# Down projection of an adaLN block: first inner product copied into the second's PSUM bank, residual gated once, and the last outer product of group 1 split by seven

## The chip, the cores and the metric

The kernel runs on one core of one Trainium2 chip. The metric is the device time of one execution in microseconds (us). The kernel before has a median of 729.99 us over three runs (731.19, 729.23, 729.99). The execution that was profiled took 729.17 us, and its span, from its first to its last instruction, is 727.4 us. Engines are named as in the profile: PE (TensorE matmuls), PEld (its weight loads), DVE (VectorE), ACT (ScalarE), POOL (GpSimd) and SP (SyncE, which here only issues DMAs).

## The reference

One transformer block on 2048 tokens of width 1024, with adaptive layer norms, linear attention of 32 heads and a gated feed-forward of inner width 3584. All inputs are bf16.

```
mod = silu(c) @ w_mod                        # six rows of 1024: sa, ca, ga, sb, cb, gb
h = layernorm(x) * (1 + ca) + sa
q, k, v = h @ wqkv ; pq, pk = phi(q), phi(k)
o = (pq @ (pk^T v)) / (pq . sum(pk))         # per head
x = x + ga * (o @ wo)
h = layernorm(x) * (1 + cb) + sb
x = x + gb * ((gelu(h @ w_gate) * (h @ w_up)) @ w_down)
```

The change is in the last line: the product with `w_down`, its gate `gb`, and the sum with `x`.

## The kernel before, in words

**Phases.** `kvq_phase` makes keys, values and queries, `merge_phase` and `wo_phase` the attention output and the first residual sum, which goes to the output tensor in HBM (`x2_scr`, a view of it). The feed-forward then runs for two groups of 1024 tokens: `gate_up(0)`, `down_out(0)`, `gate_up(1)`, `down_out(1)`.

**Products by seven.** A matrix product cut into 2x2 quadrants is computed with seven quadrant products instead of eight, on sums of quadrants of the two factors (the Strassen-Winograd scheme). In `down_out(g)` the activations of the group are cut into quadrants of 512 tokens by 1792 inner elements, and `w_down` into quadrants of 1792 by 512 columns. The seven outer products are called `b11`, `b21`, `t0`, `t1`, `b22`, `t2`, `t3`. Each of them is computed in one of two ways:

- `plain` (L1951): four row tiles of 128 tokens, each 14 matmuls of 128 x 512 into one PSUM bank, 56 wide matmuls in all.
- `nested` (L1986): again by seven, steps `g1` to `g7`, each 14 matmuls of 256 columns (two token tiles by seven inner tiles), 98 narrow matmuls in all.

Before, `t1` and `t3` of group 0 and `t3` of group 1 are plain, and all others are nested. The `t3` of group 1 is the last product of the kernel. Its fourth row tile is cut into 256, 128 and 128 columns, and the two 128-column parts go to other banks, to which ACT copies what the bank already holds (L1969).

**Steps of a nested product.** `g1` makes the first product in a bank `a`, and `fcopy` (L1097) has ACT copy it to SBUF in fp32. `g2` makes the second product in a bank of its own and hands both to `out`, where DVE adds them (`tt_op`, L791). `g3`, `g5` and `g6` continue in bank `a`, `g4` and `g7` use a bank `c`; ACT copies the results of `g3` and `g5` to SBUF, and DVE adds them in.

**What `out` does with a result.** The outer seven are joined in two fp32 tiles of SBUF, `p1v` and `p5v`, in PSUM banks 0 to 3 (into which ACT copies a partial sum so that a later plain product adds to it), and in the functions `c11_out`, `c12_out`, `c22_quads`, `c21_last`, `c21_out`. They multiply with a row of `gb` (`gate2`, `gbrow`) and either send the result to HBM with an accumulating DMA of the POOL queue (`added` and `send`, L1934), which adds it to the residual there, or, for the last 512 tokens, add it to residual rows that were loaded (`rest`, L1942) and store with a DMA of the ACT queue (`store`, L1947). Before, the gated value of a partial sum is kept too (`w12`, which lies in `p1v`) and added to the gated rest, so that `u2_out` and `u2_quads` gate once and `c12_out` gates again.

**Weight sums.** Nested products need sums of quadrants of `w_down` and of its outer sums. For the products in `LATER` (L1344) they are made in HBM (`v_scr`) by DMAs of the POOL queue, half of them accumulating (`wd_later`, L1403). They are issued piece by piece in `gate_up`, each batch behind a small POOL copy that waits for a weight load (`wd_moves`, L1353); `MOVE_AT` (L1765) has the units n of `gate_up` in which one is issued. SP loads the operands of each product into slots of SBUF (`quarters`, `W_AT`, L1910), in the order of its queue, as soon as the slot's last reader is done.

**The order of the work.** All instructions are first recorded, then put in order by a planner (`Plan`, L216), and then each engine's sequence is permuted by a table of shifts written out in the file (`SHIFTS`, L20 to L208, applied in `refine`, L470). Each engine executes its own sequence in order.

Of the kernel before, what the change touches and what calls it, by code (L numbers as in the profile page):

```python
# [11 lines left out]
BF16 = mybir.dt.bfloat16  # L12
# [495 lines left out]
def kernel(  # L508
# [1258 lines left out]
    def gate_up(g, before=()):  # L1767
# [26 lines left out]
        for n in range(NU):  # L1794
# [49 lines left out]
            if n == 0:  # L1844
                wd_todo.extend(wd_later(LATER[g + 1]))
# [390 lines left out]
```

## Time and profile before

The times are in us of the profiled execution.

| | |
|---|---|
| profiled execution | 729.17 (median of the runs 729.99) |
| span | 727.4, granted TensorE clock 1.000 |
| PE busy | 717.1 (99%), 4504 matmuls |
| DVE busy | 662.3 (91%) |
| ACT busy | 461.5 (63%) |
| POOL busy | 133.3 (18%) |
| HBM | read 128.91 MB, written 41.55 MB |
| start of `down_out(0)`, of `gate_up(1)`, of `down_out(1)` | about 402, 474, 643 |

The times of the stages in the last row are where the first matmuls of the lines L2008 and L1728 stand in the chain that ended last. Busy time of PE is the union of its matmuls; between matmuls that follow each other closely nothing is counted as idle. DVE, ACT and POOL have the line of a helper for most of their work (L791, L1097), so they are told apart by shapes and times.

### The profile page before, as it was taken

To read this page: it belongs to the slowest core of one execution; us is meant where nothing else is said; L and a number is where in the kernel's file an instruction comes from. 1 tells how busy PE (TensorE), PEld (TensorE's weight loads), DVE (VectorE), ACT (ScalarE), POOL (GpSimd) and SP (SyncE) were. 2 spreads that over 40 slices of the span, in tenths; PEclk is the share of its full clock that TensorE was granted. 3 is DMA by queue.
4 is the path that set the end of the run, shared out by engine and by line. 5 is a ranking of instruction groups with operands and counts; after the bars stand their busy time and mean duration, and the time that the engine had idled before them with its cause. 6 is when DMAs were issued, how large, how long until landed. Compare 5 with 4: busy or idle time off the path is not lost.

```text
span 727.4 us, 12503 instructions
## 1 busy us (share of the span) xinstructions
PE 717.1 (99%) x4504; PEld 417.8 (57%) x4515; DVE 662.3 (91%) x1457; ACT 461.5 (63%) x841; POOL 133.3 (18%) x210
## 2 busy tenths in 40 slices
PE   8999999999999999999999999999999999999997
PEld 4444445454444455555555787655555555568885
DVE  6698988898889999999989999898888899989998
ACT  5584665679777889998877742036777767651220
POOL 2241832011030033532221000031022100000011
PEclk9999999999999999999999999999999999999999
DMA  9967597998999797996999999786237733599994
GB/s 309 328 203 231 135 174 150 328 369 250 298 286 247 255 274 181 303 277 192 302 201 229 282 276 289 244 161 149 82 105 196 179 72 117 155 276 255 285 264 107
DMA packets 183854, 163.94 MB, mean 225 GB/s; under 512 B 34864, under 2 KB 164144, under 8 KB 183792
## 3 DMA queue, kind: packets, MB, share of 16 engines
q1 hardware_dynamic: 156880, 121.45, 57.8%
q0 software_dynamic: 25344, 40.38, 23.3%
q10 hardware_dynamic: 1568, 1.31, 0.6%
q8 instruction: 35, 0.57, 0.3%
q14 instruction: 27, 0.22, 0.1%
HBM read 128.91 MB, written 41.55 MB: 234 GB/s over the span
## 4 chain that ended last, share of the span: by engine, by line
PE 94%; DVE 2%; POOL 2%; ACT 1%; issue 1%; DMA 0%; DVEq 0%; ACTq 0%
PE psum L1728 34%; PE psum L2008 16%; PE psum L1739 11%; PE psum L1160 7%; PE psum L1230 7%; PE psum L1959 5%; PE psum L1542 4%; PE psum L1608 3%; PE psum L1259 2%; PE psum L926 2%; PE psum L1274 1%; POOL mem L877 1%; PE psum L808 1%; DVE mem L791 1%; DMA mem<-in_A_x_dram 0%
## 5 line engine op out<-in xcount | busy, mean ns | idle before, releaser
L791 DVE TENSOR_TENSOR mem<-mem 128x512 f16<-128x512 f16 (+11 forms) x837 | 383.4, 501 | 11.4 <-ACT mem L1097 2.3
L1728 PE MATMUL psum<-mem 128*128 128x512 f16 x1144 | 272.9, 379 | 0.0
L1097 ACT ACTIVATE mem<-psum 128x512 f32<-128x512 f32 (+3 forms) x327 | 171.5, 554 | 137.3 <-PE psum L2008 49.4
L791 DVE TENSOR_TENSOR mem<-psum,mem 128x512 f16<-128x512 f32 (+5 forms) x225 | 167.2, 750 | 24.4 <-PE psum L1160 4.8
L1728 PEld LDWEIGHTS <-mem 128*128 128x128 f16 (+1 forms) x1144 | 111.8, 98 | 102.7 <-issue 0.2
L2008 PE MATMUL psum<-mem 128*128 128x256 f16 (+1 forms) x1078 | 119.6, 273 | 0.0
L2008 PEld LDWEIGHTS <-mem 128*128 128x128 f16 x1078 | 105.5, 98 | 14.3
L1739 PE MATMUL psum<-mem 128*128 128x256 f16 x742 | 106.0, 273 | 0.0
L1739 PEld LDWEIGHTS <-mem 128*128 128x128 f16 (+1 forms) x742 | 72.4, 98 | 41.2 <-DVE mem L791 0.2
L1160 PE MATMUL psum<-mem 128*128 128x512 f16 (+1 forms) x273 | 62.4, 379 | 1.4 <-ACT mem L1266 0.5
L1934 POOL DMA_DIRECT2D out_dram<-mem x12 | 14.6, 1414 | 218.3 <-DVE mem L791 218.3
L1230 PE MATMUL psum<-mem 128*128 128x512 f16 x224 | 51.5, 379 | 0.0
L791 DVE TENSOR_TENSOR psum<-psum,mem 128x256 f32<-128x256 f32 x106 | 44.5, 427 | 7.5 <-ACT mem L1097 5.6
L1160 PEld LDWEIGHTS <-mem 128*128 128x128 f16 x280 | 27.2, 98 | 33.0 <-issue 1.6
L1785 ACT ACTIVATE psum<-psum 128x512 f32<-128x512 f32 x56 | 32.6, 585 | 14.7 <-PE psum L1739 8.5
L1804 ACT ACTIVATE mem<-psum 128x512 f16<-128x512 f32 x56 | 32.7, 596 | 12.3 <-PE psum L1728 12.1
L1959 PE MATMUL psum<-mem 128*128 128x512 f16 (+2 forms) x196 | 38.0, 349 | 0.0
L1230 PEld LDWEIGHTS <-mem 128*128 128x128 f16 (+1 forms) x224 | 21.6, 98 | 26.1 <-issue 0.8
L1814 ACT ACTIVATE mem<-mem 128x512 f16<-128x512 f16 x56 | 34.8, 629 | 0.3 <-DVE mem L791 0.3
L1259 PE MATMUL psum<-mem 128*128 128x512 bf16 x124 | 28.7, 379 | 1.4 <-DMA mem<-in_A_wqkv_dram 1.0
L1338 POOL DMA_DIRECT2D ts<-in_B_w_down_dram x28 | 27.6, 1165 | 11.1 <-DMA ts<-in_B_w_down_dram 11.0
L1542 PE MATMUL psum<-mem 128*128 128x512 f16 x128 | 28.3, 379 | 0.0
(148 smaller groups left out, 608.9 us busy)
## 6 DMA issues: line engine op xcount, KB each, us to landing
mem<-in_B_w_gate_dram SPq DMA_DIRECT2D x14, 1024.0 KB, 8.1
mem<-in_B_w_up_dram SPq DMA_DIRECT2D x14, 1024.0 KB
mem<-in_w_mod_dram SPq DMA_DIRECT2D x24, 512.0 KB, 7.8
mem<-us SPq DMA_DIRECT2D x24, 448.0 KB, 6.1
mem<-vs SPq DMA_DIRECT2D x20, 448.0 KB, 7.7
mem<-in_B_w_down_dram SPq DMA_DIRECT2D x18, 448.0 KB, 6.9
ts<-in_B_w_down_dram POOLq DMA_DIRECT2D x28, 256.0 KB, 5.7
mem<-ts SPq DMA_DIRECT2D x15, 448.0 KB, 8.7
```

The costliest lines, as they stand in the source:

```text
L791: ve.tensor_tensor(out=out, in0=a, in1=b, op=op)
L1097: ac.activation(out=t, in_=ps, func=AF.Copy)
L1160: te.matmul(ps, lhsT=A[:, k, i * P:(i + 1) * P], rhs=B[:, k, :], start=(start and k == 0), stop=(k == KH - 1), skip_group_check=True)
L1230: te.matmul(o, lhsT=W[:, k, (j0 + i) * P:(j0 + i + 1) * P], rhs=h_form(a, k), start=(start and k == 0), stop=(k == KH - 1), skip_group_che ...
L1259: te.matmul(ps, lhsT=hr1[b][:, k, tl * P:(tl + 1) * P], rhs=Wk[:, k, n * NW:(n + 1) * NW], start=(k == 0), stop=(k == KD - 1))
L1542: te.matmul(psw[:, half, :], lhsT=pqT[b][:, g, tl * P:(tl + 1) * P], rhs=Wp[:, g, half * NW:(half + 1) * NW], start=(g == 0), stop=(g == K ...
L1728: te.matmul(ps, lhsT=a[:, k, e, :], rhs=b[:, k, :], start=(start and k == 0), stop=(k == KH - 1), skip_group_check=True)
L1739: te.matmul(ps, lhsT=self.x[a][:, k, :], rhs=self.y[y][:, k, :], start=(start and k == 0), stop=(k == KH // 2 - 1), skip_group_check=True)
L1804: ac.activation(out=o, in_=ps, func=AF.Gelu_apprx_tanh)
L1814: ac.activation(out=o, in_=o, func=AF.Gelu_apprx_tanh)
L1959: te.matmul(psm[:, b, c], lhsT=A[:, i, q * P:(q + 1) * P], rhs=wt[:, i, c], start=(start and i == 0), stop=(i == NPR - 1), skip_group_chec ...
L2008: te.matmul(ps[:, q, :], lhsT=a[:, k, q * P:(q + 1) * P], rhs=y[:, k, :], start=(start and q == 0 and k == 0), stop=(k == NPR // 2 - 1), s ...
```

## The change

In both down phases:

- `g1` of a nested product takes a second bank `b`, and ACT copies the first product from bank `a` to bank `b`. `g2` adds its own product to that bank. DVE no longer adds the two, and the copy to SBUF is gone.
- `u2_out` and `u2_quads` no longer gate and no longer refill PSUM banks; `c12_out` adds the partial sum first and gates the sum once; `w12` is gone.

In group 1 alone:

- `t3` is nested. `sub_sums` on `A22` makes its left sums on DVE (four instructions of 128 x 1792), `v_scr` has a fourth part, and `MOVE_AT` issues 16 moves instead of 8 in `gate_up(1)`, over the units 1 to 12. Seven operand loads of 448 KB replace two of 896 KB.
- The product `t2` (`c22_quads`) no longer loads its residual and stores, but sends its result with two accumulating DMAs. Of `t3`, the first quadrant is sent in the same way (one DMA of 128 KB), the second and third are stored by half width.
- The last quadrant (`last_quad`) is made in two halves: the second half's bank is filled by an ACT copy, 7 matmuls make each half, and each half is gated, added and stored by itself.

The table `SHIFTS` is new throughout, so that the order of the instructions is another one on every engine, in all phases. The instruction counts outside the down phases and the moves are unchanged.

```diff
 SHIFTS = {
...
-    v_scr = scr_pool.tile([P, NPR // 2, 3, 4, HB], F16, name="vs", tag="vs")
+    v_scr = scr_pool.tile([P, NPR // 2, 4, 4, HB], F16, name="vs", tag="vs")
...
-    LATER = ("b11", "t2", "t1")
+    LATER = ("b11", "t2", "t1", "t3")
...
-    MOVE_AT = ((0, 1, 2, 3, 4, 5, 6, 11), (1, 2, 3, 4, 5, 6, 7, 8))
+    MOVE_AT = ((1, 1, 1, 1, 1, 1, 1, 0, 0, 0, 0, 1, 0, 0), (0, 2, 1, 1, 2, 1, 1, 2, 1, 1, 2, 1, 1, 0))
...
             if n == 0:
-                wd_todo.extend(wd_later(LATER[g + 1]))
-            if n in MOVE_AT[g]:
-                wd_moves(w_next["a11"][:, 0, 0, 0:1], 1)
+                for name in LATER[1:2] if g == 0 else LATER[2:]:
+                    wd_todo.extend(wd_later(name))
+            if MOVE_AT[g][n]:
+                wd_moves(w_next["a11"][:, 0, 0, 0:1], MOVE_AT[g][n])
...
-             "t2": (17, 18, 5, 6, 11, 12, 13), "t3": 7}]
+             "t2": (17, 18, 5, 6, 11, 12, 13), "t3": (7, 8, 9, 10, 0, 1, 2)}]
...
             def g1():
-                st["a"] = free.pop(0)
-                st["p1"] = fcopy(sub_ring, mm(st["a"], x11, y11, True))
+                st["a"], st["b"] = free.pop(0), free.pop(0)
+                mm(st["a"], x11, y11, True)
+                ac.activation(out=psm[:, st["b"], :], in_=psm[:, st["a"], :], func=AF.Copy)
 
             def g2():
-                b = free.pop(0)
-                out(0, 0, mm(b, x12, y21, True), st["p1"], ALU.add)
-                free.append(b)
+                out(0, 0, mm(st["b"], x12, y21, False), None, None)
+                free.append(st["b"])
...
             def g7():
-                out(0, 1, mm(st["c"], s4, y22, False), st["u2"], ALU.subtract)
+                if end:
+                    last_quad(st["u2"], st["c"], lambda b, q: mm(b, s4, y22, False, (q,)))
+                else:
+                    out(0, 1, mm(st["c"], s4, y22, False), st["u2"], ALU.subtract)
...
-        def u2_out(q, ps, c):
+        def u2_out(q, ps):
             tt_op(p5v[:, q, :], p5v[:, q, :], ps, ALU.subtract)
-            tt_op(w12[:, q, :], p5v[:, q, :], gbrow[:, NW:D], ALU.mult)
...
             tt_op(u, ps, u, ALU.add)
-            if (r, c) in ((1, 0), (0, 1)):
-                rows = slice(2 * r, 2 * r + 2)
-                for q in (2 * r, 2 * r + 1):
-                    ac.activation(out=psm[:, q, :], in_=p1v[:, q, :], func=AF.Copy)
-                tt_op(p5v[:, rows], p5v[:, rows], p1v[:, rows], ALU.subtract)
-                tt_op(w12[:, rows], p5v[:, rows], gbrow[:, None, NW:D].to_broadcast((P, 2, NW)), ALU.mult)
+            tt_op(v, v, u, ALU.subtract)
...
         def c12_out(xt, send):
...
-                if sb is None:
-                    tt_op(t, ps, gate2(1, c), ALU.mult)
-                else:
-                    tt_op(t, ps, sb, op)
-                    tt_op(t, t, gate2(1, c), ALU.mult)
-                tt_op(quad(xt, r, c), t, quad(w12, r, c), ALU.add)
+                if sb is not None:
+                    tt_op(sb, ps, sb, op)
+                    ps = sb
+                tt_op(t, ps, quad(p5v, r, c), ALU.add)
+                tt_op(quad(xt, r, c), t, gate2(1, c), ALU.mult)
...
-        def c22_quads(x2, x1, send=None):
+        def c22_quads(xt, send):
...
                 tt_op(t, d, ps, ALU.subtract)
-                tt_op(d, ps, gate2(0, c), ALU.mult)
...
-                tt_op(t, t, gate2(1, c), ALU.mult)
-                tt_op(quad(x2, r, c), t, quad(x2, r, c), ALU.add)
+                if last:
+                    tt_op(quad(p1v, r, c), ps, quad(p1v, r, c), ALU.add)
+                else:
+                    tt_op(d, ps, gate2(0, c), ALU.mult)
+                tt_op(quad(xt, r, c), t, gate2(1, c), ALU.mult)
                 if (r, c) in ((1, 0), (0, 1)):
-                    store(x2, 1, 1, 2 * r, 2 * r + 2)
-                tt_op(d, d, quad(x1, r, c), ALU.add)
+                    send(2 * r, 2 * r + 2)
...
+        def c21_quads(r, c, ps, sb, op):
+            t, x = f16_pair(), quad(last_x, r, c)
+            if sb is not None:
+                tt_op(sb, ps, sb, op)
+                ps = sb
+            tt_op(t, ps, quad(p1v, r, c), ALU.add)
+            if (r, c) == (0, 0):
+                xt, send = added(1, 0)
+                tt_op(quad(xt, r, c), t, gate2(0, c), ALU.mult)
+                send(0, 2, slice(0, HB))
+                return
+            tt_op(t, t, gate2(0, c), ALU.mult)
+            tt_op(x, t, x, ALU.add)
+            store(last_x, 1, 0, 2 * r, 2 * r + 2, slice(c * HB, (c + 1) * HB))
+
+        def last_quad(u2, c, mm):
+            u, x = quad(p1v, 0, 1), quad(last_x, 0, 1)
+            tt_op(u, u, u2, ALU.subtract)
+            tt_op(u, u, gate2(0, 1), ALU.mult)
+            tt_op(u, u, x, ALU.add)
+            b = free.pop(0)
+            pv = [psm[:, n, q * HB:(q + 1) * HB] for q, n in ((0, c), (1, b))]
+            ac.activation(out=pv[1], in_=psm[:, c, HB:NW], func=AF.Copy)
+            for q, n in ((0, c), (1, b)):
+                mm(n, q)
+                t = c0_ring()[:, 0:HB]
+                tt_op(t, pv[q], gbrow[:, HB:NW], ALU.mult)
+                tt_op(x[:, q], t, u[:, q], ALU.add)
+                store(last_x, 1, 0, q, q + 1, slice(HB, NW))
...
         if last:
             sub_sums(A21, sub_a, None, [slice(0, NPR // 2)])
-            x2, x1 = rest(1, 1), rest(1, 0, last_x)
-            n7 = nested("t2", A21, sub_a, None, c22_quads(x2, x1))
+            rest(1, 0)
+            n7 = nested("t2", A21, sub_a, None, c22_quads(*added(1, 1)))
             run(n7[0], n3[5], n7[1], n3[6], *n7[2:5])
-            m8 = plain("t3", A22, c21_last(x1), False)
-            run(m8[0], n7[5], m8[2], n7[6], m8[1], *m8[3:])
+            sub_sums(A22, sub_d, None, [slice(0, NPR // 2)])
+            n8 = nested("t3", A22, sub_d, None, c21_quads)
+            run(n8[0], n7[5], n8[1], n7[6], *n8[2:])
```

More of the change, by code (lines that the diff above doesn't have):

```diff
@@ L722 @@
     sub_ring = Ring(177, [2, HB], FP32, 3)
-    xio_ring = Ring(183, [TT, NW], BF16, 1)
-    xio_ring.slots += Ring(203, [TT, NW], BF16, 1).slots
     acc_ring = Ring(183, [TT, NW], F16, 1)
@@ L1931, in added, with send, rest @@
             xt = acc_ring()
-            def send(lo, hi):
+            def send(lo, hi, c=slice(0, NW)):
                 gp.dma_start(
-                    out=x2_scr[2 * g + half][lo * P:hi * P, nh * NW:(nh + 1) * NW].rearrange("(q p) n -> p q n", p=P),
-                    in_=xt[:, lo:hi], accum_op=ALU.add)
+                    out=x2_scr[2 * g + half][lo * P:hi * P, nh * NW:(nh + 1) * NW][:, c].rearrange("(q p) n -> p q n", p=P),
+                    in_=xt[:, lo:hi, c], accum_op=ALU.add)
             return xt, send
-        def rest(half, nh, xt=None):
-            xt = xio_ring() if xt is None else xt
-            sy.dma_start(out=xt, in_=x2_scr[2 * g + half][:, nh * NW:(nh + 1) * NW].rearrange("(q p) n -> p q n", p=P))
-            return xt
+        def rest(half, nh):
+            sy.dma_start(out=last_x, in_=x2_scr[2 * g + half][:, nh * NW:(nh + 1) * NW].rearrange("(q p) n -> p q n", p=P))
         def store(xt, half, nh, lo, hi, c=slice(0, NW)):
@@ L1955, in plain, with mm @@
                 sy.dma_start(out=wt[:, c], in_=wd_full[name][:, c])
-            def mm(b, q, c):
+            def mm(q):
                 for i in range(NPR):
-                    te.matmul(psm[:, b, c], lhsT=A[:, i, q * P:(q + 1) * P], rhs=wt[:, i, c],
+                    te.matmul(psm[:, q, :], lhsT=A[:, i, q * P:(q + 1) * P], rhs=wt[:, i, :],
                               start=(start and i == 0), stop=(i == NPR - 1), skip_group_check=True)
             steps = []
-            end = last and name == "t3"
-            for q in (2, 3, 0, 1) if end else range(TT):
-                parts = [(0, HB, q), (HB, 3 * P, 2), (3 * P, NW, 3)] if end and q == 1 else [(0, NW, q)]
-                for lo, hi, b in parts:
-                    c = slice(lo, hi)
-                    if b != q:
-                        steps.append(lambda c=c, b=b, q=q: ac.activation(out=psm[:, b, c], in_=psm[:, q, c], func=AF.Copy))
-                steps += [f for lo, hi, b in parts for c in (slice(lo, hi),)
-                          for f in (lambda q=q, b=b, c=c: mm(b, q, c), lambda q=q, b=b, c=c: out(q, psm[:, b, c], c))]
+            for q in range(TT):
+                steps += [lambda q=q: mm(q), lambda q=q: out(q, psm[:, q, :])]
             return steps
@@ L2002, in nested, with mm @@
             st = {}
-            def mm(b, a, y, start):
+            end = last and name == "t3"
+            def mm(b, a, y, start, qs=(0, 1)):
                 ps = psm[:, b, :].rearrange("p (q n) -> p q n", q=2)
-                for q in range(2):
+                for q in qs:
                     for k in range(NPR // 2):
@@ L2069, in p5_out @@
                 tt_op(quad(p5v, r, c), ps, sb, op)
-        w12 = p1v
         def p1_quads(r, c, ps, sb, op):
@@ L2080, in p1_quads @@
                     ac.activation(out=psm[:, q, :], in_=p1v[:, q, :], func=AF.Copy)
-        def u2_out(q, ps, c):
+        def u2_out(q, ps):
             tt_op(p5v[:, q, :], p5v[:, q, :], ps, ALU.subtract)
-            tt_op(w12[:, q, :], p5v[:, q, :], gbrow[:, NW:D], ALU.mult)
         def u2_quads(r, c, ps, sb, op):
-            u = quad(p1v, r, c)
+            u, v = quad(p1v, r, c), quad(p5v, r, c)
             if sb is not None:
@@ L2118, in out @@
                 tt_op(t, d, ps, ALU.subtract)
-                tt_op(d, ps, gate2(0, c), ALU.mult)
-                if send is not None:
-                    tt_op(quad(x2, r, c), t, gate2(1, c), ALU.mult)
-                    if (r, c) in ((1, 0), (0, 1)):
-                        send(2 * r, 2 * r + 2)
-                    return
-                tt_op(t, t, gate2(1, c), ALU.mult)
-                tt_op(quad(x2, r, c), t, quad(x2, r, c), ALU.add)
+                if last:
+                    tt_op(quad(p1v, r, c), ps, quad(p1v, r, c), ALU.add)
+                else:
+                    tt_op(d, ps, gate2(0, c), ALU.mult)
@@ L2127, in out @@
+                tt_op(quad(xt, r, c), t, gate2(1, c), ALU.mult)
                 if (r, c) in ((1, 0), (0, 1)):
-                    store(x2, 1, 1, 2 * r, 2 * r + 2)
-                tt_op(d, d, quad(x1, r, c), ALU.add)
-            return out
-        def c21_last(xt):
-            def out(q, ps, c):
-                t = c0_ring()[:, c]
-                tt_op(t, ps, gbrow[:, c], ALU.mult)
-                tt_op(xt[:, q, c], t, p5v[:, q, c], ALU.add)
-                store(xt, 1, 0, q, q + 1, c)
-            return out
+                    send(2 * r, 2 * r + 2)
@@ L2140, in c21_out, with out @@
         def c21_out(xt, send):
-            def out(q, ps, c):
+            def out(q, ps):
                 t = c0_ring()
@@ L2189, in down_out @@
             sub_sums(A21, sub_a, None, [slice(0, NPR // 2)])
-            x2, x1 = rest(1, 1), rest(1, 0, last_x)
-            n7 = nested("t2", A21, sub_a, None, c22_quads(x2, x1))
+            rest(1, 0)
+            n7 = nested("t2", A21, sub_a, None, c22_quads(*added(1, 1)))
             run(n7[0], n3[5], n7[1], n3[6], *n7[2:5])
-            m8 = plain("t3", A22, c21_last(x1), False)
-            run(m8[0], n7[5], m8[2], n7[6], m8[1], *m8[3:])
+            sub_sums(A22, sub_d, None, [slice(0, NPR // 2)])
+            n8 = nested("t3", A22, sub_d, None, c21_quads)
+            run(n8[0], n7[5], n8[1], n7[6], *n8[2:])
         else:
             sub_sums(A21, sub_d, None, [slice(0, NPR // 2)])
-            x2, send = added(1, 1)
-            n7 = nested("t2", A21, sub_d, None, c22_quads(x2, None, send))
+            n7 = nested("t2", A21, sub_d, None, c22_quads(*added(1, 1)))
             run(n7[0], n3[5], n7[1], n3[6], *n7[2:5])
```

357 rows, old and new, of the table SHIFTS are left out of this document.

## The prediction

> **What bounds the kernel now.** I read the busy times first, then the windows by stage, the waits of PE, the chain that ended last, and the timeline of the last 20 us. The page's first line of busy times and the windows (us, then busy time of PE, PEld, DVE, ACT, POOL with instruction counts, the granted clock, the DMA share, GB/s):
>
> ```profile
> PE 717.1 (99%) x4504; PEld 417.8 (57%) x4515; DVE 662.3 (91%) x1457; ACT 461.5 (63%) x841; POOL 133.3 (18%) x210
> ```
>
> ```profile
> 0.00:29.50 29.50, 25.79 (x205) 12.48 (x206) 16.38 (x60) 13.71 (x29) 3.79 (x22) 1.00 0.98 334
> 29.50:90.00 60.50, 58.23 (x320) 28.05 (x327) 57.07 (x140) 40.97 (x59) 31.02 (x58) 1.00 0.66 199
> ...
> 400.00:487.00 87.00, 87.00 (x651) 63.52 (x649) 82.46 (x142) 29.16 (x49) 7.32 (x6) 1.00 0.97 253
> 487.00:640.00 153.00, 153.00 (x891) 86.93 (x890) 136.91 (x333) 109.52 (x235) 14.07 (x18) 1.00 0.52 136
> 640.00:709.00 69.00, 69.00 (x602) 58.63 (x600) 65.45 (x103) 18.47 (x34) 2.47 (x2) 1.00 0.99 271
> 709.00:727.40 18.40, 14.28 (x108) 9.25 (x106) 15.09 (x31) 0.52 (x2) 2.42 (x2) 1.00 0.49 110
> ```
>
> PE is the bound at full clock: it is busy in every microsecond of 400 to 709, both down phases included. It idles 3.71 us before 29.5, 2.27 us from there to 90, and 4.12 us at the end. So only three things move the time: the matmul time itself, idle time in the first 90 us, and what follows the last matmul. PE's waits (in total, times, longest):
>
> ```profile
> PE psum L1259 <- DMA mem<-in_A_wqkv_dram: 1.0, 1, 1.0
> PE psum L1274 <- DVE mem L791: 0.7, 1, 0.7
> PE psum L1160 <- ACT mem L1266: 0.5, 1, 0.5
> PE psum L1160 <- ACT mem L1097: 0.5, 1, 0.5
> ```
>
> All of them lie before 90 us; no line of the down phases (L1959, L2008) is among them. The end, from the chain (start, us) and then from the timeline:
>
> ```profile
> 711.09 1.53 PE psum L2008 x14
> 712.62 3.02 PE psum L1959 x14
> ...
> 717.17 5.34 PE psum L1959 x42
> ```
>
> ```profile
> 709.27 2.42 POOL L1934 DMA_DIRECT2D out_dram<-mem  x2 [12.89 <-DVE mem L791]
> ...
> 717.00 6.28 PE L1959 MATMUL psum<-mem 128*128 128x128 f16 x56
> ...
> 723.26 0.69 DVE L791 TENSOR_TENSOR mem<-mem 128x512 bf16<-128x512 f16 x1
> 724.06 0.29 DVE L791 TENSOR_TENSOR mem<-psum,mem 128x128 f16<-128x128 f32 x1
> 724.38 0.29 DVE L791 TENSOR_TENSOR mem<-mem 128x128 bf16<-128x128 f16 x1
> ```
>
> Fourteen 256-column matmuls take 1.53 us (109 ns each) and fourteen 512-column ones 3.02 us (216 ns each). PE ends at E = 723.28, DVE at 724.67 (E+1.39), and the span ends 2.73 us after that, at E+4.12.
>
> **The change, part by part.**
>
> *Matmuls.* Group 1's `t3` was three plain tiles of 3.02 us and a fourth in pieces: 6.12 us from 717.00 to E without the 0.16 us of drain, less one wide tile, is 3.10 us. Together 12.16 us. By seven it is 7 x 1.53 = 10.71 us. Saved: 1.45 us, all on the path, since PE idles nowhere near. Every other product keeps its matmuls.
>
> *The first copy.* The copy of 128x512 from bank to bank takes 0.585 us (the ACT group of L1785) where the copy to SBUF took 0.597. What is new is that `g2`, and every matmul behind it in PE's queue, waits for it; before, only DVE did. In the new order the shortest distance from the end of `g1` to `g2` is one step of 1.53 us (`t0` and `t2` of group 1, with a `g6` between), elsewhere 2.4 us and more. ACT is busy 18.47 of 69 us there, so 0.6 us plus some 0.25 us for drain and hand-over fits. Cost taken: 0. If ACT is just inside another 0.6 us copy, 1.45 us still fits. Without cover it would be up to 0.7 us at each of twelve places.
>
> *DVE and ACT work.* Counting the instructions of both orders with 0.69 us for an fp32 128x512, 0.42 for f16, 1.22 for fp32 128x1024 and 1.09 for f16 128x1792: DVE loses 6.4 us in group 0 (nine instructions) and 4.1 us in group 1 (six on balance, with 4.35 us of `A22` sums added). ACT loses four bank refills and nine copies to SBUF and gains twelve bank copies. PE never waits for either there, so this is worth 0. `g1` holds two banks of four at once; the banks that `t2`'s `g4` and `g6` need are the tightest, where DVE arrives about when PE does: bounds 0 to 0.3 us, taken 0.
>
> *DMA.* Eight more moves of 448 KB go through POOL's queue in `gate_up(1)`, one or two per unit of 11 us, at a median of 6.4 us to landing, where the DMA share is 0.52 and POOL does nothing else that PE needs: 0. In the down phase `t3` loads 1.4 MB more, some 5 us at 271 GB/s while the share is 0.99. Its loads stand last in SP's queue, issued about 33 to 23 us before E and needed 13.6 to 1.5 us before E; the slowest landing of the sends in that stretch, 11.2 us, leaves some 7 us or more. One load of `t2` (for `g5`) now stands behind a `t3` load whose slot comes free 28.6 us before E; it is needed at E-15.1, so 13.5 us against 11.2. Taken 0.
>
> *The end.* After `t3`'s `g4` (E-3.0) DVE has eleven instructions left: two fp32 steps, then gates, sums and the two last halves. With the spacing seen in the rows (0.61 us between independent fp32 128x512, 0.72 between dependent ones, 0.34 for f16 and 256 columns) they end at E+2.0, 0.6 later than before. A store then closes the span at E+4.7: +0.6. The second candidate is new: the accumulating DMAs. The gate multiplies for the last two sends stand right before those eleven, so POOL starts the last one at about E-1.4 (0.36 us hand-over, 1.27 us for the one ahead). How long such a DMA takes is in the trace:
>
> ```profile
> DMA to landing us min/median/max: 4.2/5.5/11.2
> ```
>
> With 5.5 it lands at E+4.1, and with the 1.2 us of closing that follow the last landing the span ends at E+5.3: +1.2. With 4.2 the stores decide: +0.6. With 11.2, which belongs to the stretch with a DMA share of 0.99, +6.9. The end has a share of 0.49, so I take the middle of the first two, +0.9.
>
> The Trainium skill ("DMA: Bandwidth & Descriptors", section "Anatomy of one DMA — SWDGE (gpsimd) path") gives 2.0 us plus the bytes over 436 KB per us for such a DMA, an estimate of 2.6 us for 256 KB; by it the stores alone would close the span and the sum would be 0.3 us lower. The trace, with 4.2 us as its shortest, does not agree.
>
> *The new order of the first 90 us.* Its instructions are the same. The first layer norm's scale is ready about 0.35 us earlier (two small instructions no longer stand before it), but the keys wait for their weights, the DMA share is 0.98 up to then, and the same 8.25 MB stand before them in SP's queue: 0. For the 2.27 us of idle time from 29.5 to 90 the row is a bound for a gain; for a loss I take the same size. I take 0, since both orders have the same phases with the same reserves.
>
> **Sum.** -1.45 + 0.9 = -0.55 us. The profiled execution took 729.17, so it would take 728.6; that execution lies 0.8 below the median of the runs. Against the median of 729.99 the prediction is 729.4. A change of 0.3% (2.2 us) is about what a measurement of this kernel can tell from none.
>
> **Rivals.**
>
> 1. *The new order also removes the early idle time: faster.* For it: 2.27 us are there, in four waits for ACT, DVE and DMA that an order can move. Against it: DMA and POOL latencies set part of them. All of it gone gives 729.4 - 2.3 = 727.1; it counts as faster from 1.6 us on.
> 2. *The accumulating sends close the span late: slower.* Place: the five sends of the last 13 us, of which four are issued in the last 6. Price: the last landing beyond E+3.5 counts in full. At 11.2 us it is 6.9 - 0.9 = +6.0, 735.4. Against it: the DMA share at the end. It makes the kernel slower by over 0.3% if that DMA takes more than 9 us.
> 3. *PE waits in the down phases: slower.* For it: PE now depends on ACT at twelve places, and DVE had no idle microsecond from 700 to 722. Against it: the 1.53 us of cover. At half of the places 0.6 us gives 3.6, 733.0; decisive from 2.8 us.
> 4. *Narrow matmuls cost more per column, and the change does not do what it says.* By rows, 109.3 ns twice is 218.6 against 215.7, worth 0.14 us and already in the sum: 729.4. The Trainium skill ("TensorE: Matmul & The Clock Gate", section "Back-to-back issue gap") has sustained spacings of 81 ns at 128 columns and 131 at 512; between them 256 columns would be an estimated 98 ns, 98 of them 9.6 us against 7.3 for the plain form, and the sum would be +3.2 us, 733.2. The trace (109 and 216) does not agree.
>
> **How the numbers follow.** Forecast 0.60, rival 1 0.22, rival 2 0.08, rival 3 0.09, rival 4 0.01. So faster 0.22, same 0.60, slower 0.18. The low end of the range is rival 1 in full, 727.1. The high end, 732.2, holds the forecast with its bounds (0.3 us of bank waits, the early loss of 2.27) and the beginnings of rivals 2 and 3; what lies above and below is less than 2 in 10.
>
> **What would show it.** L2008 with 98 more matmuls at unchanged spacing, L1959 with 84 fewer, and 1.45 us less from the first matmul of `t3` to E. No PE wait on L2008. DVE's last instruction about 2.0 us after E; POOL's last L1934 issued about 1.4 us before E and landing some 4 after it, the span ending 4.7 to 5.3 after E. PE idle before 90 us near 6.0. The prediction is wrong if that idle time moves by over 1.5 us, if a down phase shows a wait of PE for ACT or DVE, or if the end after E is beyond 7 us.

## The result, and the profile after

The kernel after takes 734.69 us (median; 733.70 to 736.42) where the kernel before takes 730.07. The ratio is 1.0065, 95% interval 1.0041 to 1.0088. A second set of runs, beside the last experiments, gave 733.99 us and 1.006 (1.0048 to 1.0072). The forecast was 729.4 in a range of 727.1 to 732.2; it was wrong.

The profiled execution takes 733.70 us, with a span of 731.9. The last matmul ends at E = 725.91 (before 723.28), and the span ends at E+5.99 (before E+4.12). So 2.63 us were lost ahead of the last matmul although the matmuls need 1.5 us less, and 1.87 us behind it. The first line of the page, after:

```profile
PE 718.2 (98%) x4529; PEld 420.1 (57%) x4529; DVE 655.8 (90%) x1442; ACT 463.4 (63%) x843; POOL 148.0 (20%) x225
```

VectorE is busy 6.5 us less. It has the 15 instructions less that the prediction counted, but the prediction's two terms for them, 6.4 and 4.1 us, are too large: the times of all VectorE instructions, added up, fell by 7.4 us. PE's busy time is 1.1 us longer, with fewer columns to multiply. Half of that lies in the record: the profile of before lacks 11 of its 4515 matmuls (their weight loads are all there), seven ahead of 90 us and four from there to 135, and each leaves 0.05 us that is shown as idle and was not. The other half is real. The windows by stage, in the columns of the prediction, show a little of why. After:

```profile
90.00:240.00 150.00, 149.68 (x816) 68.39 (x815) 134.30 (x247) 107.15 (x149) 29.77 (x44) 1.00 0.89 257
240.00:400.00 160.00, 158.63 (x910) 88.82 (x909) 154.46 (x402) 139.18 (x281) 41.70 (x60) 1.00 0.91 246
...
709.00:731.90 22.90, 16.87 (x154) 14.72 (x151) 18.28 (x36) 2.74 (x5) 7.76 (x7) 0.91 0.89 168
```

Before:

```profile
90.00:240.00 150.00, 149.79 (x818) 69.26 (x821) 133.50 (x250) 108.91 (x152) 28.44 (x44) 1.00 0.93 263
240.00:400.00 160.00, 160.00 (x919) 89.67 (x918) 155.46 (x404) 140.25 (x285) 43.80 (x59) 1.00 0.92 244
```

From 240 to 400 us PE did nine matmuls fewer and idled 1.37 us: new, and far ahead of the down phases. From 90 to 240 us busy time hardly differs, yet PE falls behind there too. One must look at where a piece of work starts. The first 24 matmuls of `wo_phase` in the timeline (start, us), before and after:

```profile
186.56 5.35 PE L1542 MATMUL psum<-mem 128*128 128x512 f16 x24
```

```profile
188.47 5.35 PE L1543 MATMUL psum<-mem 128*128 128x512 f16 x24
```

They start 1.91 us later. A matmul of 512 columns counts as busy for 0.38 us, though the next one follows 0.216 us after it; a gap of up to 0.16 us between two of them is therefore not seen as idle. Four gaps of 0.17 to 0.35 us from 107 to 118 us, 0.98 in sum, showed in the list of waits as one of 0.2 us.

So the loss is better read as a *lag*: the start of a matmul, less the time that all matmuls ahead of it in PE's sequence need at 0.2156 us per 512 columns. By this count, which includes the 11 matmuls without a record, all matmuls need 727.5 us before and 1.51 less after (a few narrow forms are counted too high, in both alike). The table has each run's lag less that of the kernel before at the same time, in us. The span is then 727.4 - 1.51 + lag at E + (end after E - 4.12); for `old_new_order_2`, whose matmuls are those of before, the 1.51 falls away.

| run | at 90 us | 240 | 400 | 650 | E | end after E |
|---|---|---|---|---|---|---|
| before | 0 | 0 | 0 | 0 | 0 | 4.12 |
| after | 0.4 | 1.9 | 3.6 | 3.9 | 4.1 | 5.99 |
| after, profiled again | 1.5 | 3.0 | 4.0 | 4.2 | 4.3 | 6.34 |
| `early_a` | -0.1 | -0.2 | 0.7 | 1.7 | 1.7 | 6.49 |
| `sp_load` | 0.7 | 2.0 | 2.1 | 3.3 | 4.6 | 6.00 |
| `plain_sends` | 0.6 | 1.9 | 3.8 | 4.9 | 5.2 | 5.40 |
| `tail_order` | 1.4 | 3.2 | 3.7 | 3.7 | 4.4 | 5.13 |
| `move_late` | 2.0 | 3.5 | 4.4 | 4.4 | 5.6 | 6.81 |
| `own_tile` | 0.6 | 2.0 | 3.5 | 3.7 | 3.8 | 6.08 |
| `old_new_order_2` | 0.7 | 2.5 | 2.7 | 2.8 | 2.8 | 4.10 |
| `all_four` | -0.2 | -0.1 | 0.3 | 0.3 | 0.9 | 5.66 |
| `all_five` | 1.0 | 1.4 | 1.6 | 2.2 | 2.3 | 5.72 |

For the kernel after: 727.4 - 1.51 + 4.14 + 1.87 = 731.9. Of the 4.14, some 3.6 were lost by 400 us, where both kernels execute the same instructions in another order.

Two places can be named from the trace. From 100 to 118 us VectorE is busy for 17.63 of 18 us (before 16.43), and PE follows just behind it; that VectorE holds PE up there is read from this, not tested. And at 345 us VectorE waits for a load. The timeline of after (start, us, engine, idle time before it and what ended that):

```profile
337.02 0.38 SPq L1688 DMA_DIRECT2D mem<-in_B_w_gate_dram  x1
337.51 0.75 SPq L1374 DMA_DIRECT2D mem<-in_B_w_down_dram  x1
...
346.85 1.69 DVE L792 TENSOR_TENSOR mem<-mem 128x512 f16<-128x512 bf16 x4 [1.68 <-DMA mem<-in_B_w_down_dram]
...
349.98 1.02 PE L1729 MATMUL psum<-mem 128*128 128x512 f16 x4 [1.11 <-DVE mem L792]
```

The load of `w_down` (L1374, for `wd_sums`) is issued right behind a 1 MB load of `w_gate` and lands 9.24 us later; in the order of before it was issued at 329.86, ahead of that megabyte.

### The profile page after: what moved, and what is told of

It is laid out like the page before. It is cut to its first block, busy times and chain, and to the rows that moved or that the text cites. A ratio compares the mean times of both kernels' runs of the same rounds, so it can differ in the third digit from the quotient of the medians.

```text
span 731.9 us, 12565 instructions
## 1 busy us (share of the span) xinstructions
PE 718.2 (98%) x4529; PEld 420.1 (57%) x4529; DVE 655.8 (90%) x1442; ACT 463.4 (63%) x843; POOL 148.0 (20%) x225
## 4 chain that ended last, share of the span: by engine, by line
PE 82%; DVE 10%; DMA 5%; POOL 1%; issue 1%; ACT 1%; SPq 0%; DVEq 0%; POOLq 0%
PE psum L1729 32%; PE psum L2003 13%; PE psum L1740 10%; DVE mem L792 7%; PE psum L1161 6%; PE psum L1231 5%; PE psum L1543 4%; PE psum L1609 3%; PE psum L1959 3%; PE psum L927 2%; DMA mem<-in_B_w_down_dram 1%; DMA out_dram<-mem 1%; DMA mem<-ts 1%; DVE mem L870 1%; PE psum L1275 1%
## 5 line engine op out<-in xcount | busy, mean ns | idle before, releaser
L792 DVE TENSOR_TENSOR mem<-mem 128x256 f16<-128x256 f16 (+10 forms) x825 | 376.6, 499 | 14.0 <-DMA mem<-in_B_w_down_dram 1.7
L1098 ACT ACTIVATE mem<-psum 128x512 f32<-128x512 f32 (+3 forms) x318 | 164.5, 552 | 120.1 <-PE psum L2003 55.2
L792 DVE TENSOR_TENSOR mem<-psum,mem 128x512 f16<-128x512 f32 (+4 forms) x220 | 164.3, 755 | 22.9 <-ACT mem L1098 3.7
L2003 PE MATMUL psum<-mem 128*128 128x256 f16 (+1 forms) x1176 | 130.0, 273 | 0.0
L2003 PEld LDWEIGHTS <-mem 128*128 128x128 f16 x1176 | 115.0, 98 | 15.2 <-issue 0.2
L1936 POOL DMA_DIRECT2D out_dram<-mem x15 | 18.4, 1370 | 183.2 <-DVE mem L792 182.8
L1161 PEld LDWEIGHTS <-mem 128*128 128x128 f16 x280 | 27.1, 98 | 33.3 <-issue 1.5
L1361 POOL CAST mem<-mem 128x1 f16<-128x1 bf16 x20 | 7.5, 376 | 100.2 <-DMA mem<-in_B_w_gate_dram 48.2
```

What stands on the lines that cost most here:

```text
L792: ve.tensor_tensor(out=out, in0=a, in1=b, op=op)
L1098: ac.activation(out=t, in_=ps, func=AF.Copy)
L1161: te.matmul(ps, lhsT=A[:, k, i * P:(i + 1) * P], rhs=B[:, k, :], start=(start and k == 0), stop=(k == KH - 1), skip_group_check=True)
L2003: te.matmul(ps[:, q, :], lhsT=a[:, k, q * P:(q + 1) * P], rhs=y[:, k, :], start=(start and q == 0 and k == 0), stop=(k == NPR // 2 - 1), s ...
```

## Experiments on the order of the first 400 us

**Early phases in the old order.** On each engine the instructions recorded ahead of `gate_up(0)` are put in the order of before; every other instruction keeps its place. `early_b` does the same up to the tenth unit of `gate_up(0)`. The code is unchanged, only the table differs:

```diff
 SHIFTS = {
     "PE": (
-        "z13 8 8 2 2 2 2 -6 -6 -6 -6 z3 3 3 ..."
+        "z13 8 8 8 -3 -3 -3 -3 -3 -3 -3 -3 z3 2 2 ..."
...
```

> The kernel after, with one edit: on every engine, the instructions of `kvq_phase`, `merge_phase` and `wo_phase` stand in the order that they have before the change; all else keeps its place. Theory of the order: between 100 and 200 us the order after lets PE lag 1.9 us more than the order before (0.98 us of it in four gaps from 107 to 118 us, behind a VectorE without a pause) and 0.2 us more ahead of 90 us, so this gives 734.7 - 2.1 = 732.6 us, the stall at 349 us stays, and the last matmul ends at about 723.8 instead of 725.9. Rival, that the loss comes from the down phases and the added moves, and that the early lag is given back by later reserves: 734.7, with the last matmul at 725.9.

Measured: 733.41 us, ratio 1.0042 (1.0025 to 1.0060); 1.3 us less than the first set of runs of after and 0.6 less than the second, with intervals that overlap, where 2.1 were expected. The time alone therefore doesn't decide it. In the trace the lag of the first 240 us is gone, and `wo_phase` starts as it did before:

```profile
186.45 5.35 PE L1545 MATMUL psum<-mem 128*128 128x512 f16 x24
```

What was not expected: 0.9 us come from 240 to 400 us all the same and 1.0 more from 400 to 650 (0.3 at 439 us and 0.7 at 520 us; both are taken up below).

> As the run before it, but the order of before reaches further, through the first ten units of `gate_up(0)` (to about 350 us). Theory of the order: the 1.7 us that PE loses at 350 and 357 us go as well, so 734.7 - 3.8 = 730.9 us, the last matmul at about 722.1, and the end after it unchanged at 6.0 us. Rival, the down phases and the moves: 734.7.

Measured: 745.42 us, ratio 1.0205. Far off both theories: 11 us slower than after. At the seam between the two orders PE waits at 353 to 378 us and once at 421. The waits of `early_b`:

```profile
PE psum L1742 <- DVE psum L794: 3.8, 2, 3.5
PE psum L2005 <- ACT psum L2012: 1.8, 1, 1.8
PE psum L1742 <- ACT psum L1748: 1.5, 1, 1.5
```

Up to 350 us its lag is that of before (0.2 us), so the theory holds as far as it is tested; the seam itself makes the total useless. The wait at 421 us is for the bank copy ahead of a `g2` (`L2012`), which ACT makes late behind a step that waits for a load. And after the wait of 3.5 us the granted clock is 0.5 up to 361.6 us: matmuls of 512 columns then follow each other after 0.427 us instead of 0.216, which costs some 2 us more. Two orders that are each good can't be joined at just any place.

**The new order alone.** The other way round: the kernel before, nothing of the change, with the order of after in its first phases.

> The kernel before, with one edit: the instructions of `kvq_phase`, `merge_phase`, `wo_phase` and the first unit of `gate_up(0)` stand in the order that they have after the change; nothing of the change itself is in it. Theory of the order: PE lags by the 1.9 us that it lags by 240 us in the kernel after, so this is 0.26% above the kernel before (731.6 for 729.7), with the gaps at 107 to 118 us in its trace. Rival, that the change in the down phases causes the lag: as the kernel before.

Measured: 739.58 us, ratio 1.0138 (1.0119 to 1.0157), 10 us instead of 2. The lag at 240 us is 2.4 us, as the theory has it, but the cut lay one unit into `gate_up(0)`, and behind it PE waits 0.7 us at 262 us and once for 4.3 us at 327. The cause of the long wait in POOL's timeline (`L1341` is a move, `L1505` a small step of the layer norm that the next tile needs):

```profile
320.08 0.91 POOL L1341 DMA_DIRECT2D vs<-ts  x1 [0.17 <-issue]
329.02 1.49 POOL L1341 DMA_DIRECT2D vs<-ts  x1 [8.03 <-DMA vs<-ts]
329.80 1.30 POOL L1505 TENSOR_TENSOR mem<-mem 128x1 f32<-128x1 f32 x1
```

An accumulating move that must wait for the one before it holds up the small step queued behind it. The long wait then costs more than itself. The windows behind it have a granted clock (third number from the end) of 0.58 and 0.57:

```profile
331.00:333.00 2.00, 1.25 (x7) 0.89 (x7) 1.86 (x5) 0.58 (x1) 2.00 (x4) 0.58 1.01 116
333.00:335.00 2.00, 2.00 (x7) 0.78 (x6) 1.97 (x6) 1.78 (x4) 0.05 (x1) 0.57 1.28 219
```

Matmuls of 512 columns follow each other after 0.427 us there, and another 1.5 us are lost. By start times the lag at 400 us is 9.3 us: 2.4 at 240 us, 0.9 and 4.5 at the two waits, and the 1.5. So the cut was made again where both orders have nearly the same instructions behind it, and the POOL moves that reach into `gate_up(0)` kept their places:

> The kernel before, with the order of after in `kvq_phase` and `merge_phase` and the first `wo` work, cut at the start of `wo_phase`, where both orders have nearly the same instructions behind them; the POOL moves that are put off into `gate_up(0)` keep their places. Theory of the order: PE lags by 1.9 to 2.4 us from 120 us on, with gaps at 81, 107 to 118 us; nothing else is lost: 731.7 to 732.1 for 729.7. Rival, that the order costs nothing by itself in the kernel before: 729.7.

Measured: 731.97 us, ratio 1.0032 (1.0020 to 1.0044). That is 2.4 us on a kernel that has nothing of the change in it. `wo_phase` starts 2.5 us later than in the kernel before:

```profile
189.07 5.35 PE L1544 MATMUL psum<-mem 128*128 128x512 f16 x24
```

and among PE's waits (in total, times, longest) stands the one at 81 us, 1.2 us long in the kernel after:

```profile
PE psum L1162 <- DVE mem L793: 1.3, 1, 1.3
```

The rival, that the lag of the first 240 us comes from the down phases or the moves, falls. The new order of the first phases costs some 2 us. Adding it alone shows that in the time; taking it away shows it in the lag: from 90 to 240 us it grows by 1.2 to 1.8 us in all eight profiles of the table with the new order there, and by 0.0 to 0.4 in the three with the old one (`early_a`, `all_four`, `all_five`).

**One load in `gate_up(0)`.**

```diff
 SP's queue, gate_up(0):
   rows of t0, for wd_sums(5)
+  rows of w_down, for wd_sums(5)
   rows of x, for tile_norm
   w_gate, 1 MB
-  rows of w_down, for wd_sums(5)
```

> The kernel after, with one DMA moved: the load of `w_down` that VectorE waits for at 345 to 347 us stands in SP's queue ahead of the 1 MB load of `w_gate` that was before it. Theory of the order, for this place: it is issued at about 336.2 instead of 337.5 us, has no megabyte ahead of it and lands near 343, ahead of VectorE's need at 345.2; PE's gap of 1.27 us at 349 and most of the 0.4 at 357 go: 734.7 - 1.5 = 733.2 us. Rival, that the DMAs as a whole are late there because the queues are full: the wait goes to the `w_gate` load or to another operand, 734.7.

Measured: 734.35 us, ratio 1.0055 (1.0036 to 1.0074), too near to after to be told from it by the time. The trace tells more. SP's timeline of this run:

```profile
336.24 0.38 SPq L1376 DMA_DIRECT2D mem<-in_B_w_down_dram  x1
336.71 1.63 SPq L1498 DMA_DIRECT2D mem<-out_dram  x1
338.44 0.38 SPq L1690 DMA_DIRECT2D mem<-in_B_w_gate_dram  x1
```

VectorE no longer waits for a load there, PE has no wait at all from 335 to 365 us, and from 240 to 400 us the lag grows by 0.1 us where it grew by 1.7 in after. The other profiles of the table bear this out. In the seven that have this load as it was in after, VectorE waits 0.4 to 1.9 us for loads of `w_down` between 340 and 370 us (in four of them also, and in `tail_order` only, for the next such load, at 368 us), and from 335 to 380 us PE loses within 0.2 us of what VectorE waits: 0.3 in `early_a` with 0.4, 1.6 in after with 1.7, 1.8 in `plain_sends` with 1.9. In the three with the load moved (`sp_load`, `all_four`, `all_five`) VectorE doesn't wait for it and PE loses 0.1 us or less. So the cause is shown by the traces, for 0.3 to 1.8 us, 1.0 on average; the rival, that another load would be late instead, falls. In the profiled execution of `sp_load` 2.6 us were lost again behind it: 1.2 from 400 to 650 us, and 1.4 from there to E (after itself loses 0.5 from 400 us to E).

## Experiments on the moves and on the end

**The wait at 520 us.** In `early_a`, `sp_load` and `plain_sends` PE waits 0.7 to 0.9 us in `gate_up(1)`, behind VectorE and a `w_gate` load that takes 9.3 to 9.4 us. The chain of `early_a`:

```profile
507.75 9.30 DMA mem<-in_B_w_gate_dram
517.05 0.02 issue
517.08 0.70 DVE mem L794
```

1.4 us ahead of that load POOL issues an accumulating move that lands at 515.8; the kernel before has its moves at a slower pace. So the second move of that unit was put off:

```diff
 POOL's queue, gate_up(1):
   copy that waits for a load, move 1
-  move 2, copy, move 3, copy, moves 4 and 5, ...
+  copy, move 2, copy, moves 3 and 4, copy, moves 5 and 6, ...
```

> The kernel after, with one DMA delayed: in `gate_up(1)`, POOL issues the second, accumulating move (at 509 us, 1.7 us ahead of the 1 MB load of `w_gate` that VectorE needs at 517 to 520) one unit later, and the five moves behind it follow. Theory of the moves: in three of four profiled executions with the new order PE waits 0.7 to 1.2 us for that load at 520; that wait goes, while the stalls of the first 400 us and the end stay. So 0.5 to 0.9 us less than after at the median, and no gap of PE at 520. Rival, that the load is late by itself: the gap stays.

Measured: 734.14 us, ratio 1.0056 (1.0042 to 1.0069): as after. There is no wait at 520 in its trace, but there is none either in the two profiles of after, in `tail_order` and in `own_tile`, which have the moves as they were. The wait comes and goes between executions, and one profile can't decide it. That the moves cause it stays open.

**The sends without accumulation.** The condition reached three sends: the two of `t2` and that of `t3`'s first quadrant (the expectation counts one more).

```diff
-                    in_=xt[:, lo:hi, c], accum_op=ALU.add)
+                    in_=xt[:, lo:hi, c], **({} if last and half else {"accum_op": ALU.add}))
```

> The kernel after, where the last four sends (the two of `t2`, and that of `t3`'s first quadrant, with the one of the half before them) write without accumulating; this leaves out the residual for the tokens 1536 to 2047 that they cover. Same instructions, same bytes. Theory: the last stores wait behind accumulating packets, which fill the DMA engines from 721 to 728.5 us at only some 130 KB per us; without them the last store lands 1.5 us after its issue as in the kernel before, not 2.6, and the end after the last matmul falls from 6.0 to 5.0 us: 733.7 us. Rival, that VectorE's backlog alone sets the end: 734.7, the end at 6.0 us.

Measured: 734.12 us, ratio 1.0055 (1.0039 to 1.0072); the end is E+5.40, between the two theories. What the DMAs do in the last 14 us, after (queue, packets, MB, share of 16 engines; then the issues, count, size, median us to landing):

```profile
q0 software_dynamic: 1250, 1.07, 60.7%
q10 hardware_dynamic: 832, 0.39, 9.6%
...
out_dram<-mem POOLq DMA_DIRECT2D x3, 256.0 KB, 5.3
...
out_dram<-mem ACTq DMA_DIRECT2D x2, 64.0 KB, 2.6
```

and in `plain_sends`:

```profile
q0 software_dynamic: 1260, 1.08, 42.5%
...
out_dram<-mem POOLq DMA_DIRECT2D x3, 256.0 KB, 2.9
...
out_dram<-mem ACTq DMA_DIRECT2D x2, 64.0 KB, 2.1
```

The same bytes hold the DMA engines for 60.7% of the time when most of them accumulate, for 42.5% when 640 KB do not. The 64 KB store whose landing is on record, the last in both, takes 2.6 us to land behind the former and 2.1 behind the latter; in the kernel before, which has no send near its end, one takes 1.6. But in `plain_sends` the last packet of the sends is through at E+0.9, ahead of the issue of that store at E+2.2, so its 0.5 us above 1.6 are not theirs. A landing of 64 KB varies by that much with no send under way.

**The sends earlier.** Same instructions, another order at the end. A send of `b22` had its data ready 12.7 us before E and stood behind one that was ready at E-5.9.

```diff
 POOL's queue, the last five sends:
   b22
-  t2, b22, t3, t2
+  b22, t2, t2, t3
 VectorE, from E-6:
+  gate multiply for t2's second send
   step of last_quad, sum of t3's first quadrant, step of last_quad
+  gate multiply for t3's send
   step of last_quad
-  gate multiply for t2's second send, gate multiply for t3's send
```

> The kernel after, with the end reordered and nothing else: POOL issues the send of `b22`'s last quadrants, whose data are ready 7 us earlier, ahead of the first send of `t2`; VectorE makes the gate multiplies for the last two sends 2 us earlier. Theory of the stores behind accumulating packets: the packets are through by about 2 us after the last matmul instead of 3.7, the last store lands some 1.6 us after its issue, and the span ends 5.1 to 5.4 us after the last matmul instead of 6.0 to 6.5: 0.7 us less than after. Rival, that VectorE's work after the last matmul (2.1 us) sets the end alone: no change, 6.0 or more.

Measured: 732.73 us (732.40 to 733.04), ratio 1.0039 (1.0026 to 1.0052), 1.3 to 2 us less than after, of which the trace shows 0.9 at the end. The end is E+5.13, inside the forecast of 5.1 to 5.4, while VectorE ends at E+2.11 as in after. The last send lands at E+2.0 instead of E+3.7, ahead of the issue of the last store, which lands in 1.7 us:

```profile
713.10 2.44 POOL L1939 DMA_DIRECT2D out_dram<-mem  x2 [2.59 <-DVE mem L795]
720.77 3.68 POOL L1939 DMA_DIRECT2D out_dram<-mem  x3 [5.24 <-DVE mem L795]
...
out_dram<-mem ACTq DMA_DIRECT2D x2, 64.0 KB, 1.7
```

So the rival, that VectorE's backlog alone sets the end, falls: 0.9 of the 1.87 us behind E by this run, and 0.5 by the landing of `plain_sends`, belong to accumulating packets that the last store meets. Another 0.7 are VectorE's (E+2.1 against E+1.4). The 0.3 to 0.7 that are left have no cause shown; the last store has 64 KB where it had 32 before.

**A tile of its own for `t2`.** In some executions PE waits once more, ahead of the second half of the last quadrant. The timeline of PE in `sp_load`:

```profile
724.71 1.69 PE L2005 MATMUL psum<-mem 128*128 128x256 f16 x14 [0.90 <-ACT psum L2141]
```

and a wait of VectorE in the same run, 9 us earlier:

```profile
DVE mem L794 <- DMA out_dram<-mem: 1.2, 1, 1.2
```

It waits for a send of `b21` to land, which still reads the tile into which `t2` is to be gated. VectorE then has no reserve, frees the bank late, ACT fills it late, and PE waits.

```diff
-            xt = acc_ring()
+            xt = at(17.5, [TT, NW], F16) if last and half and nh else acc_ring()
```

> The kernel after, with one edit: the result of `t2` that is sent goes to a tile of its own and not to the one that `b21`'s sends, issued 17 us before the last matmul, still read until 8 us before it. Theory of the accumulating sends: VectorE's wait for such a send to land (0.4 us in the first profile, 0.9 to 1.2 in others) goes, VectorE is that much further when the last quadrant's second bank has to be free, and PE's wait for ACT's copy falls to under 0.2: 0.2 to 1.0 us less than after. Rival, that VectorE is only short of time by its own work: PE's wait stays as it is.

Measured: 733.33 us, ratio 1.0048 (1.0036 to 1.0060). By the time that can't be told from after. In the trace VectorE has no wait for a send after 690 us, and PE runs through from 699.81 us to E (from start to start, the wait was 0.2 us in after, 0.6 in `tail_order`, 1.1 in `move_late`):

```profile
699.81 25.71 PE L2005 MATMUL psum<-mem 128*128 128x256 f16 x234
```

One profile without the wait would not be enough, since after has one too. But over the ten profiles of the table that have the new end PE's wait goes with VectorE's wait for a send: none where VectorE waits 0 to 0.2 us, 0.2 at 0.4, 0.5 at 0.6, 0.6 at 0.9 and 1.1 at 1.2.

**All together.**

> The kernel after, unedited, once more beside the other three, for their ratios to stand against. All theories: 734.7, 1.0065 of the kernel before. Of interest are two waits that differ between executions in the runs so far: PE's wait for the load of `w_gate` at 520 us (none in the first profile, 0.7 to 1.2 in three others) and its wait for ACT's copy ahead of the second half of the last quadrant (0.2 in the first profile, up to 1.1 in others).

Measured: 733.99 us, 1.0060. Neither wait shows in this execution (the second is under 0.1 us), but PE's wait for ACT at 41 us, 1.0 in the first profile, is 1.8 here.

> The kernel after with four reorderings and no other edit: the first phases in the order of before, the load of `w_down` ahead of the load of `w_gate` in `gate_up(0)`, the moves of `gate_up(1)` delayed, and the end reordered. If the loss is in these four places, the sum is 734.7 - 2.0 - 1.5 - 0.7 - 0.7 = 729.8 us, level with the kernel before: the 1.5 us that the matmuls save pay for an end that is still 1.1 us longer and two small waits of 0.3 in the down phases. Rival, that one stall only makes room for the next: 732 or more.

Measured: 730.50 us, ratio 1.0008 (0.9991 to 1.0024), for 729.8 expected; level with the kernel before, and clear of after, whose second interval begins at 1.0048. Its windows:

```profile
90.00:240.00 150.00, 149.98 (x822) 69.18 (x821) 133.36 (x250) 109.02 (x152) 28.39 (x43) 1.00 0.94 264
240.00:400.00 160.00, 159.87 (x919) 89.54 (x918) 155.54 (x402) 139.95 (x284) 42.70 (x59) 1.00 0.91 249
```

The lag is 0.3 us at 400 and at 650 us, so the rival, that one stall makes room for the next, falls. What is left is the change by itself: 1.51 us saved, 0.5 of PE's wait in the last quadrant and 0.4 of other lag lost, and an end that is 1.54 longer: +0.9 us in the profiled span (728.3 for 727.4).

> The four reorderings of the run before it and the tile of its own. Theory: PE's wait of 0.5 us ahead of the last half goes, so 730.0 us, still level with the kernel before (within 0.3%), with the end at 5.1 to 5.7 us after the last matmul. Rival, that the end, freed of that wait, is held up by the next store: no change, 730.5.

Measured: 730.51 us, ratio 1.0017 (1.0003 to 1.0031). PE's wait is gone, as expected, and the time is not better. The profiled execution, 1.1 us above the median, lost 1.0 us by 90 us and 0.6 at 563 us instead. Its end, E+5.72, is that of `all_four`, so the rival has the time right without its reason being seen. No kernel here beats the one before.

## Why the prediction was wrong, point by point

- *What bounds the kernel.* "So only three things move the time" is the sentence that failed. PE without idle time from 90 to 709 us says that nothing can be won there, not that nothing can be lost. VectorE is busy 89% of 90 to 240 us and 97% of 240 to 400 us, and POOL's and SP's queues have loads that arrive just in time.
- *The new order of the first 90 us: 0, with bounds of 2.27 us.* This step failed twice over. It stopped at 90 us, though the order is new in all phases, and it gave both orders "the same reserves" without looking at any. The idle time ahead of 90 us was 5.91 us, near the forecast of 6.0; the test that the prediction set itself looked at the wrong stretch. In its place the runs showed 1.9 us by 240 us, 1.5 of it behind 90 us (2.3 to 2.4 us at the median when the order stands alone), and 0.9 to 1.6 us in `gate_up(0)`, in the two profiles of after, from loads of `w_down` that come late.
- *Matmuls: -1.45.* Right: 1.51 us less in the count, `t3`'s 256-column matmuls at 109 ns.
- *The first copy: 0.* Right. PE has no wait for a bank copy ahead of a `g2` in either profile of after, so rival 3 in that form falls for this order. The cover can be lost: in `early_b` PE waits 1.8 us for such a copy.
- *DVE and ACT work: 0.* Right up to the last quadrant, though VectorE's saving was put 3 us too high. The copy that fills its second bank, which the prediction did not price, makes PE wait up to 1.1 us.
- *DMA: 0.* Open for `gate_up(1)`: a wait of 0.7 to 0.9 us at 520 us in three of eight profiles with the moves where the change puts them. In `down_out(0)` PE stopped for 0.3 us at 439 us, at the matmul that first needs the second half of `t1`'s weights (also in the second profile, `early_a` and `plain_sends`, and in none of the other six of the table with the change), which was not foreseen.
- *The end: +0.9.* Measured +1.87 (2.2 in the second profile). VectorE's last instruction was right (E+2.0 forecast, E+2.1 measured), and so was the last send (forecast with 5.5 us to landing at E+4.1, measured 5.4 and E+3.7). What failed is that stores and sends were taken as two candidates, of which the later one counts. They share the DMA engines: the stores end the span, and they end it 0.5 to 0.9 us later because the sends are under way. Rival 2 had the cause and the sign, but by another path and for less than 1 us, not 6.
- *Rival 1* had the order as a possible gain; it was the loss. *Rival 4* fell, with 109 ns per narrow matmul.

The sum with what was measured: -1.51 + 3.6 (order, to 400 us) + 0.3 (439 us) + 0.2 (last quadrant) + 1.87 = 4.5 us, and 731.9 - 727.4 = 4.5.

## What to carry to other kernels

When a change brings a new order of all instructions, its price has to be looked for in every phase, those that the change leaves alone included: a bound engine that never waits has nothing to win there and all to lose, and what keeps it fed are reserves of a microsecond in queues that nobody sees in the busy times. Compare where the same piece of work starts in both traces before comparing busy shares. And where the last stores of a kernel meet accumulating sends, price what the sends under way add to the landing of the stores (here 0.5 to 0.9 us); the later of the two, each taken alone, is too little.

## What the runs showed of the hardware that was not expected

- PE's busy time grew from 717.1 to 718.2 us while its matmuls needed 1.5 us less. With 0.5 us for the 11 matmuls without a record, some 2 us of waiting lay in gaps too short to be seen as idle.
- Two waits of PE of 3.5 and 4.3 us were followed by a granted clock of 0.5: matmuls of 512 columns stood 0.427 us apart instead of 0.216 until 361.6 us (`early_b`) and 334.7 us (`old_with_new_order`), and cost some 2 and 1.5 us on top.
- The last 1.07 MB on POOL's queue hold the DMA engines for 60.7% of 14 us when nearly all of it accumulates, and 42.5% when 640 KB of it are plain writes; a send of 256 KB lands in 5.3 us in the one case and 2.9 in the other.
- The same order loses differently from execution to execution: 0.4 to 2.0 us by 90 us, 0 or 0.7 to 0.9 at 520 us, up to 1.1 us ahead of the last half quadrant. The two sets of runs of the kernel after reach from 733.0 to 736.4 us, and a single profile is not enough to price one of these waits.
